# Gate and value products of a GLU layer on two fp16 parts per operand, scaled by powers of two found on the chip, in place of two rounded fp32 parts

## The chip, the cores and the metric

The kernel runs on one core of a Trainium2 chip. The metric is the device time of one execution in microseconds (us). A core has a matrix engine (PE, whose weight loads are listed apart as PEld), two engines for elementwise work (DVE and ACT), a slower one (POOL), and queues that issue transfers (here nearly all from SP). Each engine works through its own instructions in the order in which they were written; an instruction that waits holds back all those behind it on its engine.

## The reference, cut to what matters

```python
def _attn_ref(q, k, v, proj):                 # 2 batches, 8 heads, 768 rows, 64 wide
    q_bucket, k_bucket = ...                  # 6 sign bits of q @ proj and of k @ proj
    scores = np.where(q_bucket == k_bucket, scale * q @ k.T, -1e9)
    attn = softmax(scores)                    # sum(attn) + 1e-9 under the division
    return attn @ v

x = attn_out as [1536, 512]
gate = 1.0 / (1.0 + np.exp(-(x @ w_gate)))    # w_gate, w_val: 512 x 1536
val = x @ w_val
y = gate * val @ w_out                        # 1536 x 512
h = y @ w_in                                  # 512 x 2048, piecewise square, then @ w_out2
```

`w_gate` comes 188.5 times larger than `w_val` and the others, so its values need a scale before they fit an fp16 number.

## The kernel before, in words

**Attention** (0 to about 245 us) runs over 8 pairs of heads, four of batch 0 and then four of batch 1. A pair is one *unit* of some 28 us. In it PE makes the scores (`sc`), DVE takes row maxima (L473), ACT the exponentials (`P`, L477, with a read of the accumulator behind each), PE transposes (`pt`, L502), ACT makes the upper fp16 part (`PT`, L511) and DVE the lower (L514), and PE multiplies with the values (`O`, L560). The order of all engines comes from tables (`AT`, and `AM` for the last unit): `at(t, ...)` puts a step at tick t of its unit, and everything is recorded in order of ticks. Meanwhile the next pair's `q` and `k` are prepared by DMA copies on the chip (`H<-U`, `U<-W`, `W<-H`, `H<-N`, `N<-W`), which stand in SP's queue with the loads. The values of a pair, `vr`, are loaded, their absolute maximum is taken (DVE, L523, into `vm`), sent as a row to one partition (`vrow<-vm`, DMA), reduced there and turned into a power of two (DVE, L534 to L536), and sent back to all partitions (`vm<-vrow`, DMA). For the first pair PE carries the maxima there and back in place of the two transfers.

**The gate and value layer** (about 232 to 413 us) is made of 24 *quads*: 12 weight tiles g0, v0, g1, v1 to g5, v5, each for batch 0 and batch 1. The products of a tile are made by a scheme with 7 half-size products instead of 8 (`SEQ`: the seven write the PSUM banks qa, qe, qb, qa, qb, qc, qd). A product `P(i)` is 6 matmuls of 128x384: two halves of the depth, and for each `mm3`: upper by upper part, upper by lower, lower by upper. So a quad has 42 matmuls. Three *seeds* (`seed`, ACT, L254) copy one bank to another, on which a later product goes on adding: qb<-qa ahead of P(2), qc<-qb ahead of P(5), qd<-qb ahead of P(6). `keep5` (ACT) saves qe, `sum` (DVE) adds, `act` is the tanh of gate tiles (ACT, L257).

A weight tile is made ready while earlier quads run: `a_load` (1 MB of 64-bit words in three DMAs, `wr`), `a_abs` (ACT, 2), `a_conv` (5 to 6 DVE steps that build the fp32 numbers `wt`), `a_sum` (DVE, 4 steps, `ws`), `a_hi` (ACT: the rounded upper part, 128x768 and twice 128x512) and `a_lo` (DVE: the rest). Of g0, most steps are done by POOL during attention (the generator `fw`). `on(t, ...)` puts these steps at ticks t, where one tick is one product. The upper and lower parts of the layer's input are `hB`, `lB`, `hT`, `lT`.

**Afterwards** (413 to 777 us) come the `w_out` product (`o`, `y`) and the second MLP (`p`, `z`), whose PE work the change doesn't touch; the 24 splits of `h` into two parts (`on_h`) feed the first of them.

Of the kernel before, what the change touches and what calls it, by code (L numbers as in the profile page):

```python
# [22 lines left out]
VMIN = 2.0 ** -60  # L23
# [6 lines left out]
def lsh_attention_glu_act(ctx, tc, qt, kt, v, proj, w_gate, w_val, w_out1, w_in2, w_out2, ident_d, code_d, out):  # L30
# [28 lines left out]
    cst = const.tile([128, 5], F32, name="cst")  # L59

# [18 lines left out]
    def qtile(name, dt=F32R, q2=False):  # L79
        if q2:  # L80
            return Q2[0].tile([128, S], dt, tag="q2", bufs=10, name=name)
        return keep.tile([128, S], dt, tag="qk", bufs=26, name=name)
# [6 lines left out]
    def raw4(name):  # L89
        return keep.tile([128, 512], I64, tag="wr", bufs=2, name=name)  # L90
# [7 lines left out]
    XX, BO, WO, YF = {}, {}, {}, {}  # L98

# [77 lines left out]

    def a_load(t):

        raw = WO.setdefault(t, {})["raw"] = [raw4(f"wr{h}_{t}") for h in range(2)]  # L180
# [43 lines left out]
    class Quad:  # L224
# [31 lines left out]
        def tanh(self, out, x):  # L256
            nc.scalar.activation(out=out, in_=x, func=AF.Tanh, scale=0.5)  # L257
# [83 lines left out]
    with ExitStack() as actx:  # L341
# [11 lines left out]
        def load_v(b, p, eng=nc.sync):  # L353
            vr = ap.tile([128, 2, NI * D], F32, tag="vr", name=f"vr_{b}_{p}")
# [95 lines left out]
        class Unit:  # L450
# [28 lines left out]
            def ST(self):  # L479
                vm = VM[self.b, self.p]  # L480
                if self.i // GI == 0:
                    nc.gpsimd.tensor_scalar(out=vm[:, 2:3], in0=vm[:, 1:2], scalar1=1e-9, scalar2=1.0, op0=ALU.mult, op1=ALU.mult)
                nc.gpsimd.tensor_scalar(out=self.st[:, 2], in0=self.st[:, 1], scalar1=vm[:, 1:2], scalar2=vm[:, 2:3], op0=ALU.mult, op1=ALU.add)
# [32 lines left out]

        def split_v(b, p, h):
            vr = VR[b, p]
            if h == 0:
                vm = VM[b, p] = ap.tile([128, 3], F32, tag="vm", name=f"vm_{b}_{p}")  # L520
                row = ROW[p % 2]
                VS[b, p] = [row, vm]
                nc.vector.tensor_reduce(out=vm[:, 0:1], in_=vr, op=ALU.max, axis=AX.XY, apply_absolute_value=True)  # L523
                if (b, p) != seq[0]:
                    nc.sync.dma_start(row[:, 0:128], vm[:, 0:1])
            elif h == 1:
                row, vm = VS[b, p]
                u = row.bitcast(U32)
                first = (b, p) == seq[0]
                if first:  # L530
                    nc.vector.tensor_reduce(out=row[:, 130:131], in_=idle[0:1, 3, :], op=ALU.max, axis=AX.X)
                    nc.vector.tensor_scalar(out=row[:, 129:130], in0=row[:, 130:131], scalar1=VMIN, scalar2=None, op0=ALU.max)
                else:
                    nc.vector.tensor_reduce(out=row[:, 129:130], in_=row[:, 0:129], op=ALU.max, axis=AX.X)  # L534
# [863 lines left out]
```

## Time and profile before

| | |
|---|---|
| time, median of 3 runs | 778.2 us (775.28 to 778.82) |
| the profiled execution's own time | 779.02 us |
| its span on the core | 777.2 us (1.82 us lie outside it) |
| busy, share of the span: PE, DVE, ACT, POOL | 98%, 80%, 67%, 19% |
| matmuls | 4880 |

A busy share says how much of the span an engine had an instruction under way. Matmuls overlap, so PE counts as busy also where it is filled unevenly: what a matmul costs is read from the distance between the starts of two.

### The profile page before, as it was taken

The page shows a single profiled execution, that of the slowest core. Times are in us where ns is not written, and L with a number is a line of the kernel's source. Part 1 is how long each engine was busy: PE and PEld are TensorE (multiplying, and loading weights), DVE is VectorE, ACT ScalarE, POOL GpSimd, SP SyncE. Part 2 cuts the span into 40 slices and gives each one's busy share as a digit, 9 for nine tenths or more (in the row PEclk, how much of TensorE's full clock was granted, in tenths as well). Part 3 has the DMA queues.
Part 4 walks back from the last instruction along what each step waited for, and adds up shares of the span by engine and source line. Part 5 has one row for each costly group of instructions (what it writes and reads, how often), then busy time and mean ns, then how long its engine had stood idle before and what let it go on. Part 6 is the DMA issues. An engine that isn't in the chain of part 4 may idle for free.

```text
span 777.2 us, 12993 instructions
## 1 busy us (share of the span) xinstructions
PE 757.8 (98%) x4880; PEld 690.1 (89%) x4880; DVE 621.3 (80%) x1091; ACT 520.8 (67%) x1012; POOL 145.6 (19%) x168
## 2 busy tenths in 40 slices
PE   7899998999999999999999999999999999999997
PEld 4778886888878999999999999999999998888986
DVE  5889997999977977877869958888989867666643
ACT  5899897989875566566555543556666667676753
POOL 5345476664684000000000000000000000000000
PEclk9999999999999999999999999999999999999999
DMA  8645456454101131131122412433332201000002
GB/s 231 174 125 151 102 157 175 93 153 112 33 1 55 55 110 55 55 109 55 55 82 87 146 66 82 136 109 109 108 105 86 82 0 75 8 1 0 1 1 81
DMA packets 41390, 66.48 MB, mean 86 GB/s; under 512 B 5744, under 2 KB 28656, under 8 KB 41328
## 3 DMA queue, kind: packets, MB, share of 16 engines
q1 hardware_dynamic: 40592, 64.97, 28.4%
q8 instruction: 38, 0.62, 0.3%
q10 hardware_dynamic: 736, 0.69, 0.3%
q14 instruction: 24, 0.20, 0.1%
HBM read 45.58 MB, written 3.15 MB: 63 GB/s over the span
## 4 chain that ended last, share of the span: by engine, by line
PE 67%; DVE 1%; POOL 0%; ACT 0%; issue 0%; POOLq 0%
PE qa L290 3%; PE qa L289 3%; PE qa L291 3%; PE p L291 3%; PE p L289 3%; PE p L290 3%; PE qb L289 2%; PE y L289 2%; PE y L290 2%; PE y L291 2%; PE qe L289 2%; PE qe L290 2%; PE qe L291 2%; PE qb L290 2%; PE qb L291 2%; PE qa L1157 2%
## 5 line engine op out<-in xcount | busy, mean ns | idle before, releaser
L514 DVE SCALAR_TENSOR_TENSOR PT<-pt,PT 128x512 f16<-128x512 f32 x144 | 95.1, 680 | 9.1 <-ACT PT L511 8.3
L473 DVE TENSOR_REDUCE st<-sc 128x1 f32<-128x768 f32 x96 | 90.9, 947 | 8.2 <-PE sc L465 7.2
L511 ACT ACTIVATE PT<-pt 128x512 f16<-128x512 f32 x144 | 82.5, 599 | 14.5 <-PE pt L502 13.3
L477 ACT ACTIVATE P<-sc,st 128x768 f32<-128x768 f32 x96 | 87.0, 907 | 6.6 <-DVE st L473 5.9
L502 PE MATMUL pt<-ident,P 128*128 128x128 f32 x576 | 78.9, 278 | 0.8 <-DVE PT L514 0.8
L502 PEld LDWEIGHTS pt<-ident,P 128*128 128x128 f32 x576 | 65.9, 142 | 9.4 <-issue 4.7
L560 PE MATMUL O<-PT,vh 128*64 128x256 f16 x576 | 53.9, 277 | 0.0
L291 PE MATMUL p<-yh,whl_i 128*128 128x384 f32 x128 | 43.0, 336 | 0.0
L289 PE MATMUL p<-yh,whl_i 128*128 128x384 f32 x128 | 42.9, 335 | 0.0
L290 PE MATMUL p<-yl,whl_i 128*128 128x384 f32 x128 | 42.9, 335 | 0.0
L560 PEld LDWEIGHTS <-vh 128*64 128x64 f16 x576 | 31.3, 109 | 11.6 <-issue 10.3
L1134 ACT ACTIVATE t<-p,cst 128x384 f32<-128x384 f32 x32 | 18.3, 573 | 27.0 <-PE p L291 27.0
L560 PE MATMUL O<-PT,vl 128*64 128x256 f16 x288 | 33.8, 273 | 0.0
L465 PE MATMUL sc<-H,H 128*128 128x384 f32 x96 | 29.2, 385 | 3.6 <-DMA H<-N 3.3
L465 PE MATMUL sc<-N,N 128*128 128x384 f32 x96 | 29.4, 387 | 2.0 <-ACT N L403 1.0
L1139 DVE SCALAR_TENSOR_TENSOR gg<-p,t 128x384 f32<-128x384 f32 x32 | 17.7, 553 | 13.4 <-ACT t L1136 13.3
L254 ACT ACTIVATE qb<-qa 128x384 f32<-128x384 f32 x24 | 11.4, 475 | 24.1 <-PE qa L291 13.5
L254 ACT ACTIVATE qd<-qb 128x384 f32<-128x384 f32 x24 | 11.4, 475 | 23.8 <-PE qb L291 20.4
L374 POOL TENSOR_TENSOR W<-n,U 128x768 fp32r<-128x768 f32 x14 | 26.6, 1897 | 0.4
L135 ACT ACTIVATE w<-wr_i 128x512 f32<-128x512 f32 x16 | 10.7, 668 | 22.7 <-DMA wr_i<-in_moe_w_in_dram 22.6
L465 PE MATMUL sc<-U,U 128*128 128x384 f32 x96 | 25.0, 342 | 0.0
L289 PEld LDWEIGHTS p<-yh,whl_i 128*128 128x128 f32 x128 | 24.0, 188 | 0.5
(1219 smaller groups left out, 2486.6 us busy)
## 6 DMA issues: line engine op xcount, KB each, us to landing
wr_o<-in_moe_w_out_dram SPq DMA_DIRECT2D x28, 512.0 KB, 3.3
H<-U SPq DMA_DIRECT2D x28, 192.0 KB, 3.7
wr_i<-in_moe_w_in_dram SPq DMA_DIRECT2D x8, 512.0 KB, 3.9
wr_i<-in_moe_w_in_dram SPq DMA_DIRECT2D x16, 256.0 KB, 3.0
n<-in_qt_dram SPq DMA_DIRECT2D x8, 384.0 KB, 4.2
n<-in_kt_dram SPq DMA_DIRECT2D x8, 384.0 KB, 6.0
vr<-in_v_dram SPq DMA_DIRECT2D x8, 384.0 KB, 3.6
wr_g<-in_moe_w_gate_dram SPq DMA_DIRECT2D x6, 512.0 KB, 3.7
```

What stands on the lines that cost most here:

```text
L254: nc.scalar.activation(out=self.new("bcd"[m]), in_=src, func=AF.Copy)
L289: nc.tensor.matmul(ps, lhsT=wh, rhs=rh, start=first, stop=False, **kw)
L290: nc.tensor.matmul(ps, lhsT=wh, rhs=rl, start=False, stop=False, **kw)
L291: nc.tensor.matmul(ps, lhsT=wl, rhs=rh, start=False, stop=last, **kw)
L374: nc.gpsimd.tensor_tensor(out=self.t4[j][1], in0=self.nat[j], in1=f(self.t4[j][0]), op=ALU.subtract)
L465: nc.tensor.matmul(self.sc[:, n, 0:HN], lhsT=M[:, ts], rhs=K[:, n * HN:(n + 1) * HN], start=s0, stop=not s0)
L473: nc.vector.tensor_reduce(out=self.st[:, 0, self.c:self.c + 1], in_=self.sc[:, :, 0:HN], op=ALU.max, axis=AX.XY, negate=True)
L477: nc.scalar.activation(out=self.P, in_=self.sc[:, :, 0:HN], func=AF.Exp, bias=self.st[:, 0, self.c:self.c + 1], scale=1.0, accum_out=self. ...
L502: nc.tensor.transpose(self.ps[m][:, j, :], un[2 * self.n + e].P[:, a, c:c + 128], ident)
L511: nc.scalar.activation(out=self.part(0, m), in_=self.ps[m], func=AF.Copy, scale=PSCALE)
L514: nc.vector.scalar_tensor_tensor(out=self.part(1, m), in0=self.ps[m], scalar=PSCALE, in1=self.part(0, m), op0=ALU.mult, op1=ALU.subtract)
L560: nc.tensor.matmul(O_ps[r, 0:GN], lhsT=vv[m][:, e, i * D:(i + 1) * D], rhs=PT[:, l, e * NI + i, :], start=(s == 0), stop=(s == len(steps) ...
```

## The change

Both operands of the gate and value products become pairs of fp16 numbers (`qpair`, `w4pair`: upper and lower part in one tile, which takes the bytes that one fp32 part took). Therefore every weight tile gets a power of two of its own. `a_norm` (ACT, 128x1024) takes the absolute values of `wt` and adds them up per partition, `row_out` sends the 128 sums to one partition, `a_row` takes their maximum and its exponent (DVE, two instructions), makes the scale and its inverse (POOL, two) and sends both to all partitions, `a_hi` and `a_lo` multiply by the scale as they split, and `a_scale` (POOL) prepares the factor by which tanh and the splits of `h` take it out again. For g0, POOL multiplies `wt` once instead.

The values get one scale per batch. Batch 0's four loads stand at the start, ahead of g0's load, and their four maxima (`v_max`) are taken in unit 0; batch 1's loads and maxima are spread over units 0 to 3, and one row is sent there and back. The reductions and the two transfers of each later pair are gone, and units 4 to 6 have no `v_max`. The tables `QP` and `WP` set the ticks of a quad's and of a tile's steps; `QP` holds what stood there before.

```diff
@@ new functions
+    def exponents(row, mx, lead):
+        u = row.bitcast(U32)
+        m, e, inv, sc = (u[:, i:i + 1] for i in (128, 129, 130, 131))
+        nc.vector.tensor_reduce(out=row[:, 128:129], in_=mx, op=ALU.max, axis=AX.X)
+        nc.vector.tensor_scalar(out=e, in0=m, scalar1=EXP, scalar2=None, op0=ALU.bitwise_and)
+        nc.gpsimd.tensor_scalar(out=inv, in0=e, scalar1=EMIN, scalar2=(lead - 14.0) * 2.0 ** 23, op0=ALU.max, op1=ALU.add)
+        nc.gpsimd.tensor_scalar(out=sc, in0=inv, scalar1=-1.0, scalar2=254.0 * 2.0 ** 23, op0=ALU.mult, op1=ALU.add)
+    def row_out(key, x):
+        RW[key] = next(nrow)
+        nc.sync.dma_start(RW[key][:, 0:128], x)
+    def row_in(key, x, lead):
+        row = RW.pop(key)
+        exponents(row, row[:, 0:128], lead)
+        nc.sync.dma_start(x, row[:, 130:132].unsqueeze(1).broadcast_to([1, 128, 2]))
+    def a_norm(t):
+        x, raw = wsc[:, a_num(t)], WO[t]["raw"][0]
+        nc.scalar.activation(out=raw.bitcast(F32), in_=WO[t]["wt"], func=AF.Abs, accum_out=x[:, 0:1])
+        row_out(t, x[:, 0:1])
+    def a_row(t):
+        row_in(t, wsc[:, a_num(t), 2:4], 0.0)
@@ a_hi, a_lo, tanh
-        nc.scalar.activation(out=a_tile(t, "h" + g, q2)[:, cs], in_=WO[t][src][:, cs], func=AF.Copy)
+        nc.scalar.activation(out=a_tile(t, "h" + g, q2)[:, cs], in_=WO[t][src][:, cs], func=AF.Copy, scale=scale)
-        xsub(eng, a_tile(t, "l" + g, q2)[:, cs], WO[t][src][:, cs], f(WO[t]["h" + g][:, cs]))
+            nc.vector.scalar_tensor_tensor(out=lo, in0=x, scalar=a_sc(t), in1=hi, op0=ALU.mult, op1=ALU.subtract)
-            nc.scalar.activation(out=out, in_=x, func=AF.Tanh, scale=0.5)
+            nc.scalar.activation(out=out, in_=x, func=AF.Tanh, scale=a_out(self.t, self.b))
@@ attention: values
+        def v_max(b, p):
+            nc.vector.tensor_reduce(out=vmx[b][:, p:p + 1], in_=VR[b, p], op=ALU.max, axis=AX.XY, apply_absolute_value=True)
+        def v_all(b):
+            x = vmx[b]
+            nc.vector.tensor_reduce(out=x[:, NP:NP + 1], in_=x[:, 0:NP], op=ALU.max, axis=AX.X)
...
-            load_v(*seq[0], nc.sync)
+            for p in range(NP):
+                load_v(0, p, nc.sync)
             a_load("g0")
...
+                    t0 = AT["MAX"][2]
+                    for i in range(NP):
+                        at(t0 + 0.001 + 0.3 * i, 0, q, v_max, 0, i)
+                    at(t0 + 1.0, 0, q, v_all, 0)
...
+            at(14.05, 0, last, a_norm, "v0")
             at(14.1, 0, last, a_load, "g1")
@@ ticks of a tile's steps
-        on(base - (1.9 if t == 2 else 3.4), a_abs, n, 0, True)
...
+        on(base + T["norm"], a_norm, n)
+        on(base + T["row"], a_row, n)
+        on(base + T["scale"], a_scale, n)
...
-    on_split(t, 1.0, ("h", b, ORD[s]), lambda: HR[b, ORD[s]], lambda: hg(f"h{b}_{ORD[s]}"))
+    on_split(t, 1.0, ("h", b, ORD[s]), lambda: HR[b, ORD[s]], lambda: hg(f"h{b}_{ORD[s]}"), a_out(f"v{ORD[s] % F1H}", b))
```

**DVE in unit 0.** Before, behind the third score maximum of the first pair (`st<-sc`) there is one maximum of values (`vm<-vr`), and the fourth score maximum comes next:

```order
L473 TENSOR_REDUCE st_0_1_0_191<-sc_0_0_0_206 128x1
L523 TENSOR_REDUCE vm_0_216<-vr_0_175 128x1
L473 TENSOR_REDUCE st_0_1_0_191<-sc_0_0_1_227 128x1
L531 TENSOR_REDUCE vrow_93<-idle 1x1
L532 TENSOR_SCALAR vrow_93<-vrow_93 1x1
L535 TENSOR_SCALAR vrow_93<-vrow_93 1x1
L536 TENSOR_SCALAR vrow_93<-vrow_93 1x1
```

In the changed kernel the same place holds four maxima of values and one over the four:

```order
L549 TENSOR_REDUCE st_0_1_0_200<-sc_0_0_0_215 128x1
L591 TENSOR_REDUCE vmx_67<-vr_0_178 128x1
L591 TENSOR_REDUCE vmx_67<-vr_1_180 128x1
L591 TENSOR_REDUCE vmx_67<-vr_2_182 128x1
L591 TENSOR_REDUCE vmx_67<-vr_3_184 128x1
L595 TENSOR_REDUCE vmx_67<-vmx_67 128x1
L549 TENSOR_REDUCE st_0_1_0_200<-sc_0_0_1_235 128x1
L587 SCALAR_TENSOR_TENSOR PT_0_0_244<-pt_2_230,PT_0_0_244 128x4x128
L194 TENSOR_REDUCE row_71<-idle 1x1
L195 TENSOR_SCALAR row_71<-row_71 1x1
```

Three 128x768 reductions and one short one now stand between the third and the fourth score maximum.

**SP at the start.** Before, one load of values stands ahead of g0's three weight loads (`wr_g`) and the two copies `H<-U` for pair 1:

```order
L355 DMA vr_0_175<-in_v_dram 128x2x384
L183 DMA wr_g_177<-in_moe_w_gate_dram 128x4x128
L185 DMA wr_g_178<-in_moe_w_gate_dram 128x2x128
L186 DMA wr_g_178<-in_moe_w_gate_dram 128x2x128
L443 DMA H_0_1_148<-U_0_1_146 64x768
```

In the changed kernel there are four:

```order
L431 DMA vr_0_178<-in_v_dram 128x2x384
L431 DMA vr_1_180<-in_v_dram 128x2x384
L431 DMA vr_2_182<-in_v_dram 128x2x384
L431 DMA vr_3_184<-in_v_dram 128x2x384
L252 DMA wr_g_186<-in_moe_w_gate_dram 128x4x128
L254 DMA wr_g_187<-in_moe_w_gate_dram 128x2x128
L255 DMA wr_g_187<-in_moe_w_gate_dram 128x2x128
L519 DMA H_0_1_151<-U_0_1_149 64x768
```

Three loads of 384 KB moved ahead of the weights and of pair 1's copies.

**ACT in a gate tile's two quads** (g1 for batch 0, then the head of batch 1). Before, the second seed (`qc<-qb`) is followed by the first tanh (`h<-qa`) and the third seed (`qd<-qb`); the value tile's upper parts (`ha_v`, `hs_v`) stand between later steps:

```order
L254 ACTIVATE qc_3992<-qb_3974 128x384
L257 ACTIVATE h_1_3965<-qa 128x384
L254 ACTIVATE qd_4011<-qb_3974 128x384
L257 ACTIVATE h_1_3965<-h_1_3965 128x384
L214 ACTIVATE ha_v_4027<-wt_v_3934 128x768
```

In the changed kernel, batch 0's quad has the value tile's norm (128x1024) between the second seed and the tanh:

```order
L330 ACTIVATE qc_3968<-qb_3944 128x384
L213 ACTIVATE wr_v_3790,wsc<-wt_v_3845 128x1024
L333 ACTIVATE h_1_3935<-qa,wsc 128x384
L330 ACTIVATE qd_3988<-qb_3944 128x384
```

And batch 1's quad has two upper parts there:

```order
L330 ACTIVATE qc_4044<-qb_4024 128x384
L284 ACTIVATE a_v_4052<-wt_v_3845,wsc 128x768
L284 ACTIVATE s_v_4054<-ws_v_3966,wsc 128x512
L333 ACTIVATE h_1_4015<-qa,wsc 128x384
L330 ACTIVATE qd_4065<-qb_4024 128x384
```

So what ACT does between the second and the third seed grew by one long instruction in one quad and by two in the other.

## Rows read from the trace of the kernel before

**Rows 1.** Page, part 1: busy time of each engine.

```profile
PE 757.8 (98%) x4880; PEld 690.1 (89%) x4880; DVE 621.3 (80%) x1091; ACT 520.8 (67%) x1012; POOL 145.6 (19%) x168
```

**Rows 2.** Window of four quads: length, busy time (instructions), clock, DMA share, GB/s.

```profile
280.00:309.10 29.10, 29.10 (x170) 29.10 (x169) 23.20 (x42) 17.12 (x34) 0.00 (x0) 1.00 0.23 73
```

**Rows 3.** Timeline of PE and PEld in a quad: start, length, instruction.

```profile
284.42 0.33 PE L289 MATMUL qb<-hT,hs_v 128*128 128x384 f32 x1
...
285.46 0.33 PE L289 MATMUL qa<-hB,ha_v 128*128 128x384 f32 x1
...
284.59 0.19 PEld L291 LDWEIGHTS qb<-hT,ls_v 128*128 128x128 f32 x1
```

**Rows 4.** Warming matmuls of bf16: timeline, durations by source line, and their window.

```profile
4.47 1.30 PE L615 MATMUL idle<-bt 128*128 128x384 bf16 x7
...
L615 PEld LDWEIGHTS <-bt x25: 96/147/151, 1.1 to 14.1; 128*128 128x128 bf16 x25
L615 PE MATMUL idle<-bt x25: 326/497/543, 1.1 to 14.4; 128*128 128x384 bf16 x25
...
4.40:5.00 0.60, 0.60 (x6) 0.34 (x5) 0.04 (x1) 0.53 (x1) 0.00 (x0) 1.00 1.10 279
```

**Rows 5.** Timeline of PE: fp16 matmuls of the values, two side by side.

```profile
102.85 0.28 PE L560 MATMUL O<-PT,vl 128*64 128x256 f16 x2
...
103.40 0.28 PE L560 MATMUL O<-PT,vh 128*64 128x256 f16 x2
```

**Rows 6.** Windows of one unit each in attention, columns as in rows 2.

```profile
57.80:86.00 28.20, 27.85 (x266) 23.21 (x266) 27.92 (x48) 24.99 (x52) 13.42 (x17) 1.00 0.53 135
114.00:142.00 28.00, 24.72 (x222) 21.01 (x220) 21.45 (x35) 22.22 (x47) 15.18 (x18) 0.94 0.65 171
```

**Rows 7.** Tiles of the values: count, ns min/median/max, first and last start.

```profile
L523 DVE TENSOR_REDUCE vm<-vr x8: 939/942/944, 16.9 to 192.5; 128x1 f32<-128x768 f32 x8
...
L535 DVE TENSOR_SCALAR vrow<-vrow x8: 141/142/142, 19.1 to 200.6; 1x1 uint32<-1x1 uint32 x8
...
DMA to landing us min/median/max: 1.9/2.4/5.1
```

**Rows 8.** Timeline of DVE in unit 0, with the idle time ahead.

```profile
16.94 0.94 DVE L523 TENSOR_REDUCE vm<-vr 128x1 f32<-128x768 f32 x1
17.80 0.95 DVE L473 TENSOR_REDUCE st<-sc 128x1 f32<-128x768 f32 x1
...
26.02 0.69 DVE L514 SCALAR_TENSOR_TENSOR PT<-pt,PT 128x512 f16<-128x512 f32 x1 [1.21 <-ACT PT L511]
```

**Rows 9.** Window of the start, columns as in rows 2.

```profile
12.00:16.00 4.00, 3.73 (x16) 2.52 (x15) 2.75 (x3) 2.48 (x5) 3.83 (x4) 0.68 0.98 322
```

**Rows 10.** Timeline of PE and DVE where unit 4 begins.

```profile
120.32 0.94 PE L465 MATMUL sc<-H,H 128*128 128x384 f32 x2 [3.28 <-DMA H<-N]
...
119.78 0.28 DVE L534 TENSOR_REDUCE vrow<-vrow 1x1 f32<-1x129 f32 x1 [2.62 <-DMA vrow<-vm]
```

**Rows 11.** ACT in the quads: timeline.

```profile
285.65 0.47 ACT L254 ACTIVATE qc<-qb 128x384 f32<-128x384 f32 x1 [0.55 <-PE qb L291]
287.73 0.47 ACT L254 ACTIVATE qd<-qb 128x384 f32<-128x384 f32 x1 [1.60 <-PE qb L291]
288.12 0.84 ACT L214 ACTIVATE ha_g<-wt_g 128x768 fp32r<-128x768 f32 x1
```

**Rows 12.** ACT by source line: count, ns min/median/max, first and last start.

```profile
L214 ACT ACTIVATE hs_v<-ws_v x12: 626/626/635, 249.3 to 394.2; 128x512 fp32r<-128x512 f32 x12
...
L477 ACT ACTIVATION_READ_ACCUMULATOR P<-sc,st x96: 189/202/272, 14.7 to 228.6; 128x1 f32 x96
...
L1134 ACT ACTIVATE t<-p,cst x32: 561/568/586, 516.5 to 639.1; 128x384 f32<-128x384 f32 x32
```

**Rows 13.** Timeline of ACT at the end of attention.

```profile
237.39 0.49 ACT L257 ACTIVATE h<-qa 128x384 f32<-128x384 f32 x1 [0.58 <-PE qa L291]
...
248.53 0.84 ACT L214 ACTIVATE ha_v<-wt_v 128x768 fp32r<-128x768 f32 x1
```

More of the change, by code (lines that the diff above doesn't have):

```diff
@@ L22 @@
 PSCALE = 2.0 ** 12
-VMIN = 2.0 ** -60
+EMIN = 67.0 * 2.0 ** 23
+EXP = 0x7F800000
 TINY = 1.2e-38
@@ L59, in lsh_attention_glu_act @@
     cst = const.tile([128, 5], F32, name="cst")
+    vmx = [const.tile([128, 8], F32, name=f"vmx{b}") for b in range(B)]
+    xinv = const.tile([128, B], F32, name="xinv")
+    wsc = const.tile([128, 2 * (F1 // 2), 8], F32, name="wsc")
+    rows = [const.tile([1, 136], F32, name=f"row{i}") for i in range(3)]
     def constants():
@@ L515, in LO, with v_row, v_scale @@
                 free.append(self.bt[m])
+        def v_max(b, p):
[3 more added lines that the diff above has]
+            nc.vector.tensor_reduce(out=x[:, NP:NP + 1], in_=x[:, 0:NP], op=ALU.max, axis=AX.X)
+            if b == 0:
+                nc.tensor.transpose(idle[0:1, 3, :], x[:, NP:NP + 1], ident)
+            else:
+                row_out("x", x[:, NP:NP + 1])
+        def v_row(b):
+            if b == 0:
+                exponents(rows[0], idle[0:1, 3, :], 2.0)
+                nc.tensor.matmul(idle[:, 2, 0:2], lhsT=ones, rhs=rows[0][:, 130:132], start=True, stop=True)
+            else:
+                row_in("x", vmx[b][:, NP + 2:NP + 4], 2.0)
+        def v_scale(b):
+            if b == 0:
+                nc.scalar.copy(out=vmx[b][:, NP + 2:NP + 4], in_=idle[:, 2, 0:2])
+            nc.gpsimd.tensor_copy(out=xinv[:, b:b + 1], in_=vmx[b][:, NP + 2:NP + 3])
         def split_v(b, p, h):
@@ L519, in split_v @@
             if h == 0:
[L520 to L525, printed above, removed]
-            elif h == 1:
[L527 to L534, printed above, removed]
-                nc.vector.tensor_scalar(out=u[:, 130:131], in0=u[:, 129:130], scalar1=0x7F800000, scalar2=None, op0=ALU.bitwise_and)
-                nc.vector.tensor_scalar(out=u[:, 132:133], in0=u[:, 130:131], scalar1=-1.0, scalar2=268.0 * 2.0 ** 23, op0=ALU.mult, op1=ALU.add)
-                if not first:
-                    nc.sync.dma_start(vm[:, 1:2], row[:, 132:133].broadcast_to([1, 128]))
-                    VS[b, p][1] = vm[:, 1:2]
-            elif h == 2:
-                nc.gpsimd.tensor_scalar(out=vr, in0=vr, scalar1=VS[b, p][1], scalar2=1.0, op0=ALU.mult, op1=ALU.mult)
-            elif h == 3:
@@ L588, in first_weights @@
                     yield
+                a_norm("g0")
+                yield
+                a_row("g0")
                 a_load("v0")
+                yield
+                wt = WO["g0"]["wt"]
+                nc.gpsimd.tensor_scalar(out=wt, in0=wt, scalar1=a_sc("g0"), scalar2=1.0, op0=ALU.mult, op1=ALU.mult)
                 for m in range(4):
@@ L607, in lsh_attention_glu_act @@
             constants()
-            ROW = [ap.tile([1, 134], F32, tag=f"vrow{i}", bufs=1, name=f"vrow{i}") for i in range(2)]
-            for row in ROW:
-                nc.vector.memset(row[:, 128:129], VMIN)
             idle = pA.tile([128, 4, 128], F32, tag="pv", bufs=PVB, name="idle")
@@ L615, in warm @@
                     nc.tensor.matmul(idle[:, 0:3], lhsT=bt[:, 0:128], rhs=bt, start=True, stop=True)
-            def scale_out():
-                nc.tensor.transpose(idle[0:1, 3, :], VS[seq[0]][1][:, 0:1], ident)
-            def scale_in():
-                nc.tensor.matmul(idle[:, 2, 0:1], lhsT=ones, rhs=VS[seq[0]][0][:, 132:133], start=True, stop=True)
-            def scale_keep():
-                vm = VM[seq[0]]
-                nc.scalar.copy(out=vm[:, 1:2], in_=idle[:, 2, 0:1])
-                VS[seq[0]][1] = vm[:, 1:2]
             warm(18)
@@ L1225, in lsh_attention_glu_act @@
+        for i, g in enumerate("abcd"):
+            on(s0 + T["sum"][i], q_op, k, "sum", g)
+            on(s0 + T["act"][i] + (1.0 if k == 1 and g == "a" else 0.0), q_op, k, "act", g)
     for t in range(2, NT):
         base, n = 14 * (t - 1), name(t)
+        T = WP[n if n in WP else n[0]]
         if t > 2:
-            on(base - 9.0, a_load, n)
-        on(base - (1.9 if t == 2 else 3.4), a_abs, n, 0, True)
-        on(base - 1.4, a_abs, n, 1, True)
-        for m, d in enumerate((0.1, 0.9, 1.7, 2.4, 3.0, 3.6)):
+            on(base + T["load"], a_load, n)
```

167 lines of the change are left out of this document (109 added, 58 removed).

## The prediction

> **What bounds the kernel now.** I read three views. First the busy time of each engine: PE has work under way in 98% of the span [rows 1]. That alone would mislead, since an average covers stages with different limits, so the windows of single stages come next. In the gate and value layer, four quads take 29.10 us, and in all of that time PE and PEld are busy at a granted clock of 1.00 (2.4 GHz), while DVE has 23.2 us of work and ACT 17.1 [rows 2]. Three more windows of the same length, up to 396.4 us, read alike. So this stage lasts as long as its matmuls, and a cheaper matmul shows in the time at once. A unit of attention is another matter: in 28.2 us DVE has 27.92 us of work, PE 27.85 and ACT 24.99 [rows 6]. There three engines wait for each other in turn, and work taken from one of them comes back only in part. The third view, the timeline, gives the prices below. The layers after 413 us have the same matmuls before and after.
>
> **The matmuls: −10.6 us.** In a quad, PE starts seven matmuls between 284.42 and 285.46 us: six steps, 173.3 ns each [rows 3]. What an fp16 matmul of the same shape (128x384) takes is not shown, but two rows come near. The warming matmuls are 128x384 in bf16, a format as wide as fp16, each with a weight load: seven from 4.47 us take 1.30 us, the last of them 326 ns, so the starts lie (1.30 − 0.326) / 6 = 162.3 ns apart, at a clock of 1.00, and a load takes 96 ns where the fp32 one takes 190 [rows 3, 4]. The fp16 matmuls of the values do 256 columns in 110 ns ((103.40 − 102.85) / 5) [rows 5]; 384 columns at that rate are 165 ns. I take the first, being of the same shape: 11.0 ns × 42 matmuls = 0.46 us a quad. 23 of the 24 quads lie in the stage that PE bounds (the first lies in attention's tail), so 23 × 0.46 = 10.6 us. The bounds: 8.0 us at 165 ns, and nothing if the format makes no difference.
>
> The Trainium skill ("TensorE: Matmul & The Clock Gate", section "Back-to-back issue gap") gives for an isolated warm stream N/2.4 + 2.5 ns whatever the format, which for 384 columns is 162.5. The bf16 rows agree with it; the fp32 rows, at 173.3, do not. By that rule alone the matmuls would cost the same before and after and the sum below would end near 781 in place of 770.5.
>
> **Seeds in the quads: +1.3 us (0 to 3).** The first thing that can take the gain back is ACT, which works in order. A tick becomes 6 × 0.162 = 0.97 us. I count from the start of P(2) (284.42). The second seed starts 0.19 us after P(2) ends, as it does now (285.65 against 284.42 + 1.04) [rows 3, 11]: 1.16, and ends at 1.63. In batch 1's quad of a gate tile there then come the value tile's parts, 0.84 and 0.63 us [rows 11, 12], and the tanh, 0.49 [rows 13], each with a scale that is now read from memory. Such an operand has its nearest row in the rectifier with a bias from memory: 0.568 us for 128x384, against 0.47 for a plain copy [rows 11, 12], so 0.09 each. That makes 1.63 + 0.93 + 0.72 + 0.58 + 0.47 = 4.33 for the third seed's end, and P(6) wants it at 4 × 0.974 = 3.90. Neighbours on ACT overlap (288.12 is 0.08 before 287.73 + 0.47 [rows 11]), so some 0.33 of the lateness goes away: PE waits 0.1 to 0.43 us, once for each of v1 to v5. Middle 0.26 × 5 = 1.3 us. In batch 0's quad the norm stands there: 128x1024 with an accumulator. It is not shown; below it lies the 128x768 part (0.84) with the read of an accumulator (0.2), above it two 128x512 parts (1.26) with that read [rows 11, 12], so 1.04 to 1.46. With 1.25 the third seed ends at 1.63 + 1.25 + 0.58 + 0.47 = 3.93 less overlaps, just in time, so nothing; with both ends and the chain's other steps I keep 0 to 3 us for the stage.
>
> Hidden by the rest of this stage: DVE gains per four quads two row reductions and two 1x1 steps, 2 × (0.28 + 0.14) = 0.8 us [rows 7, 10], and ACT two norms and the scales, some 3.5; DVE has 5.9 us free and ACT 12.0 [rows 2]. The lower parts become one instruction of the same length class (0.69 for 128x512 [rows 8]). POOL does nothing there [rows 2], so the short scales are free. Without that cover the DVE steps would cost 0.8 × 5 = 4 us. The splits of h with a scale add 24 × 0.09 = 2.2 us to an ACT that has a third of the span free [rows 1].
>
> **Start of attention: +2.7 us (1.4 to 3.7).** Between the third and the fourth score maximum DVE has one maximum of values now; the next instruction follows 0.86 us after its start (17.80 − 16.94) [rows 8]. Three more cost 2.6 us and the short one over four columns about 0.1. Behind them wait the fourth score maximum, then ACT's exponential, then PE's transposes. DVE is idle later for 1.21 us, waiting for ACT [rows 8]; ACT would be just as late, so I don't subtract it, but 2.6 − 1.2 = 1.4 is the lower bound. At the same time three loads of 384 KB move ahead of g0's weights and of pair 1's copies. The transfers are full there (0.98 of their time, 322 GB/s [rows 9]), so each takes 1.2 us: 3.7 us for the copies that the next pair's first scores need. The two delays run side by side and aren't added.
>
> **Units 1 to 6: −2.1 us.** Units 1 and 2 lose the row's three DVE steps, 0.28 + 2 × 0.14 = 0.56 each [rows 7, 10], with the two transfers: 1.1 us, of which I count half, as PE has 27.85 of 28.2 us [rows 6]: −0.6. Units 4 to 6 lose the value maximum as well: 3 × (0.86 + 0.56) = 4.3 us of DVE [rows 7, 8]; half again, −2.3 with the transfers gone from SP's queue (0 to −4.3). Unit 3 keeps everything, and gets g0's norm on ACT and its row. Where unit 4 begins, PE waits 3.28 us for a copy `H<-N` and DVE 2.62 us for the row, both landing behind 1 MB of v0's weights [rows 10]; that window has 24.72 us of PE work in 28 [rows 6]. That load still stands there, three queue places from those copies, so I let the wait stay, and add +0.8 (0 to 1.5) for a norm of 1.25 us on an ACT that is nearly as full as the others.
>
> **End of attention: +1.0 us (0.3 to 2.5).** v0's norm comes behind the first tanh (237.39) [rows 13], and then its row goes out, is reduced, and comes back, each transfer 2.4 us, or 5.1 behind a large load [rows 7]; here g1's 1 MB stands between them. 237.9 + 1.25 + 2.4 + about 1 + 5.1 = 247.7 at least, and DVE's reduction stands ahead of attention's last steps. v0's upper parts start at 248.53 now [rows 13]; I count on 0.5 to 1.5 us later.
>
> **The sum.** −10.6 + 1.3 + 2.7 − 0.6 − 2.3 + 0.8 + 1.0 = −7.7 us. The profiled execution takes 779.02 us (span 777.2 and 1.82 outside it), so 771.3; the median shown is 0.8 lower, so **770.5 us**.
>
> **The rivals.** *The format makes no difference* (0.08). For it speaks that the row of another format is only seven matmuls long; against it, that the fp16 rows give 165 too. Then the 10.6 is gone: 781, no change.
> *The new steps on ACT and the rows take most of the gain back* (0.16). ACT's order leaves the third seed at 3.9 to 4.3 ticks' worth of time where 3.90 is wanted, and a wait of 0.4 us in each of 23 quads, say because another seed falls behind a norm or a tanh too, costs 8 us beyond the 1.3: 775 to 779, within 0.5%.
> *Attention gives back all that DVE loses* (0.16). DVE is the fullest engine of a unit [rows 6]. Then units 4 to 6 bring 4.3 and the wait of rows 10, with the row's small transfers no longer among the copies, shrinks by 1 to 2: 770.5 − 2.0 − 2 = 766.5, with a shorter start 764.
> *Slower* (0.10). Every `a_row` stands on DVE in order and waits for its row. If a row lands after 5.1 us, as the slowest one did, in place of 2.4 (the median) [rows 7], DVE stands still for 2.7 us, and behind it wait the sums that free PE's banks. DVE's spare time is (5.9 − 0.8) / 2 = 2.5 us a tile, but not where the wait is; if PE loses 1.5 us a tile, 11 tiles cost 16.5: 787. It ends above the time before from 0.7 us a tile on (7.7 / 11), and above 0.5% slower from 1.05.
>
> **How the numbers follow.** The forecast has the rest, 0.50, and its own range is 767 to 774 (±3.5 from the start, the end and the seeds). A measurement of this kernel can tell about 0.5%, 3.9 us, from no change: below 774.3 is faster, above 782.1 slower. Faster: 0.50 + 0.16, and 0.02 of the second rival's near end: 0.68. Same: 0.08 + 0.14 = 0.22. Slower: 0.10. From 764 to 780 all of the forecast and of the third rival, the second, and a part of the first lie inside; what is left out is the last one and the rest of the first.
>
> **What would show it.** In the changed kernel's timeline of PE: starts of fp16 matmuls 162 to 165 ns apart, and windows of four quads of 27.3 us plus 0.1 to 0.4 us of PE waiting for ACT's qd. At the start: the fourth score maximum (now at 17.80) near 20.5. In units 4 to 6: DVE's work 1.4 us less each, the unit 0.7 shorter. At v0: its upper parts at 249 to 250. I would be wrong above all if the starts lay 173 ns apart, if PE waited in every quad, or if the chain of maxima at the start moved the rest by less than 1 or more than 4 us.

## The result and the profile after

The changed kernel takes 782.33 us (median of 6 runs, 780.99 to 784.06), the kernel before 776.74 in the 6 runs now at hand: a ratio of 1.0069, with a 95% interval from 1.0048 to 1.0090. It is slower by 0.7%, where 7.7 us less (770.5) was forecast and the range ended at 780. The profiled execution took 782.72 us with a span of 780.9; that of before, 779.02.

First the step on which the forecast rested. The page's busy times, which answer to [rows 1]:

```profile
PE 752.0 (96%) x4880; PEld 614.8 (79%) x4880; DVE 626.2 (80%) x1094; ACT 539.6 (69%) x1036; POOL 155.5 (20%) x203
```

And the timeline of PE in a quad, to set beside [rows 3]:

```profile
293.00 0.33 PE L367 MATMUL qc<-pB,s_v 128*128 128x384 f16 x1
293.17 0.33 PE L365 MATMUL qd<-pT,a_v 128*128 128x384 f16 x1
293.33 0.33 PE L366 MATMUL qd<-pT,a_v 128*128 128x384 f16 x1
293.49 0.33 PE L367 MATMUL qd<-pT,a_v 128*128 128x384 f16 x1
```

Three steps in 0.49 us: an fp16 matmul starts every 163 ns, where the fp32 one took 173. The cheaper matmul is there. It isn't in the time. The windows of [rows 2], and one with more in it, show why:

```profile
280.00:309.10 29.10, 28.13 (x172) 16.63 (x171) 24.40 (x47) 20.21 (x40) 2.69 (x8) 1.00 0.23 73
...
338.20:367.30 29.10, 26.90 (x165) 15.87 (x163) 23.63 (x46) 19.00 (x37) 1.85 (x5) 1.00 0.24 73
```

PE was busy in all of these 29.10 us before. Now it stands still for 1 to 2.2 us of each window. The waits of PE from the end of attention to the end of the quads (225 to 420 us), each with what it waited for, the sum, the number and the longest:

```profile
PE qb L365 <- ACT qb L330: 6.0, 9, 1.5
PE qd L365 <- ACT qd L330: 1.4, 2, 1.3
PE qa L365 <- ACT a_g L284: 1.2, 1, 1.2
PE qb L365 <- ACT qc L330: 0.8, 2, 0.5
PE pt L575 <- DVE PT L587: 0.8, 2, 0.5
PE qa L367 <- DVE a_g L294: 0.7, 1, 0.7
```

Apart from `pt`, which stood there before, these are waits for seeds and for a gate tile's parts: 10.1 us, where the same list of before has 1.3 (0.95 for ACT's qb and 0.3 for POOL's hT). The list is short of the loss: it counts a wait only from the end of the matmul drawn ahead of it, and that end lies 0.17 us behind the place where the next could have started (0.33 us long, 163 ns apart). The starts give all of it. Here is the first matmul of a quad's second product (`qe`), in the second quad and in the last, before and then after:

```profile
245.02 0.47 PE L289 MATMUL qe<-hT,hs_g 128*128 128x384 f32 x1
407.13 0.33 PE L289 MATMUL qe<-hT,hs_v 128*128 128x384 f32 x1
...
246.74 0.33 PE L365 MATMUL qe<-pT,s_g 128*128 128x384 f16 x1
410.73 0.33 PE L365 MATMUL qe<-pT,s_v 128*128 128x384 f16 x1
```

These 22 quads take 162.11 us before and 163.99 after. A quad in which PE never waits takes 7.28 us before and 6.825 after (42 matmuls, 173.3 and 162.5 ns apart), so 22 × 0.455 = 10.0 us are saved. The rest is lost: 1.9 us before and 13.8 after, 11.9 more. Of the 13.8, 7.4 us fall in the 18 quads from the sixth on, where nothing was lost before, and 6.4 in the four ahead of them, where 1.9 were.

What goes wrong in a steady quad is in ACT's timeline (start, length, instruction):

```profile
286.74 1.04 ACT L213 ACTIVATE wr_g<-wt_g 128x1024 f32<-128x1024 f32 x1
287.68 0.19 ACT L213 ACTIVATION_READ_ACCUMULATOR wr_g<-wt_g 128x1 f32 x1
287.78 0.60 ACT L333 ACTIVATE h<-h,wsc 128x384 f32<-128x384 f32 x1
288.28 0.56 ACT L333 ACTIVATE h<-qd,wsc 128x384 f32<-128x384 f32 x1
288.75 0.47 ACT L330 ACTIVATE qb<-qa 128x384 f32<-128x384 f32 x1
```

The *next gate* tile's norm stands among the tanh steps that end a gate tile's second quad, and the first seed of the next quad comes behind all of them. The matmul behind it waited, 0.54 us by the list and 0.70 by the distance of its start from the one before:

```profile
289.27 0.32 PE L365 MATMUL qb<-pT,s_v 128*128 128x384 f16 x1 [0.54 <-ACT qb L330]
```

I had put the value tile's norm and parts into the sum, and not this one.

The start lost more than forecast. DVE, then ACT, to set beside [rows 8], and PE's first scores of pair 1 (at 37.51 before):

```profile
16.50 3.52 DVE L591 TENSOR_REDUCE vmx<-vr 128x1 f32<-128x768 f32 x4
20.06 0.16 DVE L595 TENSOR_REDUCE vmx<-vmx 128x1 f32<-128x4 f32 x1
...
21.11 0.90 ACT L553 ACTIVATE P<-sc,st 128x768 f32<-128x768 f32 x1 [3.01 <-DVE st L549]
...
20.27 0.27 PE L597 MATMUL idle<-ident,vmx 128*1 128x128 f32 x1 [1.12 <-DVE vmx L595]
22.65 0.58 PE L604 MATMUL idle<-row,ones 1*128 1x2 f32 x2 [1.68 <-POOL row L197]
...
43.01 0.42 PE L541 MATMUL sc<-H,H 128*128 128x384 f32 x1
...
24.00:26.00 2.00, 2.00 (x11) 0.56 (x10) 0.69 (x1) 1.61 (x4) 0.87 (x2) 0.50 1.07 389
```

The fourth score maximum, behind the four, came at 20.13 in place of 17.80, as worked out (2.3 us). But pair 1 began 5.5 us late. The last row, a window, shows what else there is: PE runs at a granted clock of 0.50 (1.2 GHz) from 15.4 to 18.8 us and again, behind the two waits, from 22.2 to 29.1. The first of these stretches begins ahead of the waits, and the three other profiled kernels with this start (experiments 2 to 4) have a clock of 1.00 there; it falls once in each, from 20 to 22 us on, and they begin pair 1 at 41.96 to 42.51, so 4.5 to 5.0 us late. And one part went better: PE waits 1.51 us for `H<-N` at unit 4 in place of 3.28 [rows 10].

### The profile page after: what moved, and what is told of

The parts are those of the page before. It is cut to its first block, busy times and chain, and to the rows that moved or that the text cites. A ratio compares the mean times of both kernels' runs of the same rounds, so it can differ in the third digit from the quotient of the medians.

```text
span 780.9 us, 13074 instructions
## 1 busy us (share of the span) xinstructions
PE 752.0 (96%) x4880; PEld 614.8 (79%) x4880; DVE 626.2 (80%) x1094; ACT 539.6 (69%) x1036; POOL 155.5 (20%) x203
## 3 DMA queue, kind: packets, MB, share of 16 engines
q1 hardware_dynamic: 42320, 64.98, 28.2%
## 4 chain that ended last, share of the span: by engine, by line
PE 56%; ACT 6%; DVE 2%; DMA 1%; issue 1%; POOL 0%; ACTq 0%; DVEq 0%
PE p L367 3%; PE p L365 3%; PE p L366 3%; PE y L365 2%; PE y L366 2%; PE y L367 2%; PE qa L367 2%; PE qa L366 2%; PE qa L365 2%; PE qa L1233 2%; PE qa L1232 2%; PE qe L1232 2%; PE qe L1233 2%; PE qa L1231 2%; PE qe L1231 2%; PE o L1232 2%
## 5 line engine op out<-in xcount | busy, mean ns | idle before, releaser
L635 PEld LDWEIGHTS <-vh 128*64 128x64 f16 x576 | 31.3, 109 | 11.8 <-issue 10.3
L196 POOL TENSOR_SCALAR row<-row 1x1 uint32<-1x1 uint32 x14 | 3.7, 264 | 119.3 <-DVE row L195 119.3
L365 PEld LDWEIGHTS p<-yh,whl_i 128*128 128x128 f32 x128 | 24.0, 188 | 0.5
L366 PEld LDWEIGHTS p<-yl,whl_i 128*128 128x128 f32 x128 | 24.0, 188 | 0.5
L367 PEld LDWEIGHTS p<-yh,whl_i 128*128 128x128 f32 x128 | 24.0, 188 | 0.0
```

Of the source, the lines that this page charges most:

```text
L365: nc.tensor.matmul(ps, lhsT=wh, rhs=rh, start=first, stop=False, **kw)
L366: nc.tensor.matmul(ps, lhsT=wh, rhs=rl, start=False, stop=False, **kw)
L367: nc.tensor.matmul(ps, lhsT=wl, rhs=rh, start=False, stop=last, **kw)
L635: nc.tensor.matmul(O_ps[r, 0:GN], lhsT=vv[m][:, e, i * D:(i + 1) * D], rhs=PT[:, l, e * NI + i, :], start=(s == 0), stop=(s == len(steps) ...
```

## The experiments

**1. The values as before.** The attention part of the change undone (`load_v`, `split_v` with its own row for each pair, PE's row for the first pair); `xinv` is 1.

```diff
-            for p in range(NP):
-                load_v(0, p, nc.sync)
+            load_v(*seq[0], nc.sync)
...
-                        at(t0 + 0.001 + 0.3 * i, 0, q, v_max, 0, i)
...
+                    vs[:2] = AT["MAX"][2] + 0.001, AT["MAX"][3] + 0.001
```

> The fp16 products and the tables of the change, but the values scaled per pair of heads as before (the factor per batch that tanh takes out is then a constant 1). Theory 'start': the four maxima and the row at the start cost the 5.5 us by which pair 1's first scores came later, and 2.3 us of that came back where units 4 and 5 begin; so undoing this part brings about 3 us: 779. Pair 1's scores begin near 37.5 us again, and PE waits 3 us for H<-N at unit 4 again. Rival 'the quads alone': the start's delay is absorbed by attention's end, so nothing changes by more than 1 us: 782.

775.93 us (10 runs), 0.9989 of the time before [0.9976, 1.0002], so 6.4 us below the changed kernel. Pair 1's scores begin here:

```profile
37.07 0.42 PE L543 MATMUL sc<-H,H 128*128 128x384 f32 x1
```

The lead over the changed kernel is 5.94 us there, the same when unit 3 begins (96.24 against 90.30), and 6.2 us when the quads do. So the start's loss is never given back, and units 4 to 6, which lost 4.3 us of DVE work, gained nothing by it: from unit 4's first scores to unit 7's it is 78.89 us in the changed kernel and 78.83 here. The shorter wait at unit 4 is there as well (1.3 us): it isn't the values that shortened it. By SP's order it is v0's load, which now stands behind g0's row and so behind one of the two copies; no run moved that load alone. Both my expectation (3 us) and its rival (none) were too small.

**2 and 3. The quads without the search, and with the norm alone.** In the second the norm stays, and the row and its two transfers are left out as well as the DVE and POOL steps.

```diff
     def constants():
+        nc.gpsimd.memset(wsc[:, :, 2:4], 1.0)
...
     def a_norm(t):
-        x, raw = wsc[:, a_num(t)], WO[t]["raw"][0]
-        nc.scalar.activation(out=raw.bitcast(F32), in_=WO[t]["wt"], func=AF.Abs, accum_out=x[:, 0:1])
-        row_out(t, x[:, 0:1])
+        pass
     def a_row(t):
-        row_in(t, wsc[:, a_num(t), 2:4], 0.0)
+        pass
```

```diff
     def constants():
+        nc.gpsimd.memset(wsc[:, :, 2:4], 1.0)
...
-        row_out(t, x[:, 0:1])
     def a_row(t):
-        row_in(t, wsc[:, a_num(t), 2:4], 0.0)
+        pass
```

> The changed kernel without the search for the weights' powers of two: no norm, no row, no transfers, a constant scale of 1 read from the same memory operands. Theory 'chain': the norm on ACT and the wait for the row stand ahead of seeds and cost most of the 8.7 us that PE lost in the quads; without them the stretch from the second quad to the end of the quads shrinks from 171.3 to about 164 us and the time falls by 6 to 8: 775. Rival 'operands': the scale operands and the places of the upper parts in ACT's order are to blame; then at most 2 us come back: 780 to 782.

> The changed kernel with the norm on ACT but without the row (no transfers, no DVE and POOL steps; constant scale). Within the theory 'chain' it tells the norm from the row. If the norm's place on ACT is the price, PE still waits 0.54 us for the first seed behind it in each of five quads, and the gain over the changed kernel is 3 to 4 us (779); if the wait for the row is the price, nearly all of what the kernel without the search gains is here too (within 1 us of it).

Without the search: 775.84 us, 0.9979 [0.9966, 0.9992]; with the norm alone 779.12, 1.0020 [1.0003, 1.0037]. The 22 quads take 158.73 and 162.33 us (163.99 in the changed kernel). In both runs PE's granted clock is 0.50 for 3.4 us in the first quads (271.0 to 274.4 and 272.8 to 276.2), behind waits much like those of the changed kernel, where the clock stayed at 1.00; so the 18 quads from the sixth on compare better. They take 123.57 us without the search, 127.02 with the norm alone and 130.24 in the changed kernel: the norms cost 3.45 us and the rows 3.2, and the medians of the times agree (3.3 and 3.2). (The expectation's stretch reaches to the first matmul of the `w_out` product; it is 171.3 us in the changed kernel, 166.1 and 169.7 here.) The kernel without the search has this window of four quads, with PE busy throughout and 180 matmuls in it where 170 stood:

```profile
280.00:309.10 29.10, 29.10 (x180) 17.49 (x179) 24.84 (x46) 19.31 (x38) 0.00 (x0) 1.00 0.23 73
```

With the norm alone, PE's waits between 276 and 408 us are four for the first seed:

```profile
PE qb L365 <- ACT qb L330: 2.3, 4, 0.6
```

The rival that blamed the scale operands falls: both kernels still read them, and without the search hardly a wait is left in the steady quads (0.3 us by the list).

**4. The same work, re-timed.** Nothing is taken out; six entries in two rows of the table of ticks move.

```diff
-        "g": {... "norm": -1.456, "row": 1.893, "scale": 7.914, ... "hi": (6.968, 7.625, 8.56), "lo": (7.021, 8.161, 9.79)},
+        "g": {... "norm": 1.0, "row": 4.5, "scale": 9.0, ... "hi": (8.05, 9.0, 10.05), "lo": (8.9, 10.1, 11.0)},
-        "v": {... "hi": (10.245, 10.388, 12.351), ...},
+        "v": {... "hi": (10.245, 12.0, 12.9), ...},
```

> The changed kernel, complete, with three rows of the table of ticks altered: the norm of a gate tile after the first seed of the next quad in place of ahead of it, its row and upper parts 1 to 2.5 ticks later, and the value tile's half-size upper parts behind the third seed. Theory 'order': what PE loses are places in ACT's order, not ACT's work, so PE's waits in the steady quads (0.12 + 0.54 + 0.3 to 1.5 us in four quads) go and the time falls by 4 to 5: 778. Rival 'work': ACT and the rows are simply too long; the waits turn up behind other instructions and the time stays within 1 us of 782.

776.78 us, 1.0002 [0.9987, 1.0016]: 5.6 us less than the changed kernel, a little more than expected. PE's waits between 276 and 408 us:

```profile
PE qb L365 <- ACT qb L330: 0.4, 1, 0.4
PE qb L365 <- ACT qc L330: 0.3, 1, 0.3
```

The 18 quads from the sixth on take 124.66 us, 5.6 less than in the changed kernel with all its work, and 1.1 more than without the search. So it is order and not work. It isn't ACT's order alone, though: with the gate tile's row later, the value tile's 1 MB load stands ahead of the outgoing row, no longer between it and the scale that comes back, and the ten scales of these quads land after 2.32 to 2.44 us, where in the changed kernel those of g2 to g5 took 2.8 to 4.1. Experiments 3 and 9 hold the two shares apart.

**5 and 6. The clock at the start, and the row's steps on DVE.** One execution each.

```diff
+                    at(t0 + 0.999, 0, q, warm, 4)
                     at(t0 + 1.0, 0, q, v_all, 0)
+                    at(AT["T"][1] + 0.0005, 0, q, warm, 6)
```

```diff
-    def exponents(row, mx, lead):
+    def exponents(row, mx, lead, eng=nc.gpsimd):
...
-                exponents(rows[0], idle[0:1, 3, :], 2.0)
+                exponents(rows[0], idle[0:1, 3, :], 2.0, nc.vector)
```

> The changed kernel with ten more warming matmuls, four and six of them, where PE waits at the start for the maxima and for the row. They do no work that is used. Theory 'clock': the start lost 5.5 us and not 2.7 because PE, left idle by the maxima, fell to 1.2 GHz (granted clock 0.50 from 16 to 18 and from 24 to 28 us); if PE is kept busy the clock stays up and pair 1's first scores come 2 us earlier, near 41. Rival 'row': the loss lies in the waits of the chain itself; the clock rises but pair 1's scores stay at 42.5 to 43.5.

> The changed kernel, but the first row's two steps on POOL are done by DVE, as they were before the change. Theory 'row': PE waits 1.68 us for POOL there; on DVE the two steps take 0.3 us in place of 0.7, and pair 1's first scores come 0.5 to 1 us earlier: 42.2. Rival 'maxima alone': ACT's exponential, 3 us late behind the four maxima, sets the pace, and nothing moves: 43.0.

With the warming matmuls the run took 778.25 us, and pair 1 began at 40.22, 2.8 us earlier than in the changed kernel and 1.7 to 2.3 earlier than in the three others with its start (41.96 to 42.51), whose clock fell only once. Profiles with one start and one clock differ by up to 1.3 us at pair 1 (36.10 to 37.41 in the three with the values as before), so the size is rough. And not all of the 4.1 us below the median is the start's: the 22 quads, which these matmuls don't touch, took 162.7 us here in place of 164.0. The windows from 14 to 38 us of the changed kernel and of this one:

```profile
14.00:38.00 24.00, 18.95 (x94) 14.56 (x94) 16.86 (x27) 15.43 (x33) 9.42 (x15) 0.79 0.76 215
```

```profile
14.00:38.00 24.00, 18.84 (x127) 14.18 (x127) 19.39 (x30) 16.42 (x34) 9.44 (x15) 1.00 0.79 210
```

The busy time of PE is equal, the matmuls are 94 and 127, ten of them the added ones: the clock is 0.79 in one and 1.00 in the other. In the three others with this start it is 0.86. The waits of the chain stay (0.96 and 1.11 us). With the row on DVE the run took 781.68 us and pair 1 began at 41.96, as in experiment 4 where POOL does the steps: it says nothing either way.

**7. The maxima spread.** One value maximum behind each of four steps, the row later and on DVE.

```diff
-                        at(t0 + 0.001 + 0.3 * i, 0, q, v_max, 0, i)
-                    at(t0 + 1.0, 0, q, v_all, 0)
+                        at((t0 + 0.001, 1.92, 2.72, 3.40)[i], 0, q, v_max, 0, i)
+                    at(3.42, 0, q, v_all, 0)
...
+                    at(4.27, 0, q, v_row, 0)
```

> The changed kernel with the first batch's four maxima spread: one behind each of the score maxima and lower parts that follow, the row later and on DVE, so that no score maximum waits for more than one of them. The loads stand as in the change. Theory 'maxima in front of a score maximum': pair 1's first scores come at 39.5 to 40.5, 2.5 to 3.5 us earlier than in the changed kernel, and the time falls as much: 779. Rival 'loads': the three loads ahead of pair 1's copies set the start; then it stays near 43.

Pair 1 began at 39.95, 3.1 us earlier (in three more kernels with this start at 40.78 to 42.19), and yet the time is 782.16, 1.0071 [1.0056, 1.0086]. Part of the 3.1 is the clock, which was at 0.50 for 3.4 us here and for 10.3 in the changed kernel. The other three have it there for 6.8 us, as have the three others with the start of the change (41.96 to 42.51), so the spread itself brought some 1 us, no more than such profiles scatter. The gain was lost again at 350 us, where ACT, then PE, wait; the two issues on SP that matter stand first:

```profile
343.58 0.46 SPq L255 DMA_DIRECT2D wr_v<-in_moe_w_val_dram  x1
...
345.06 0.51 SPq L209 DMA_DIRECT2D wsc<-row  x1
...
350.22 0.93 ACT L284 ACTIVATE a_g<-wt_g,wsc 128x768 f16<-128x768 f32 x1 [2.67 <-DMA wsc<-row]
...
352.74 0.32 PE L365 MATMUL qb<-pT,s_v 128*128 128x384 f16 x1 [2.53 <-ACT qb L330]
...
353.40:356.80 3.40, 3.40 (x12) 1.65 (x11) 2.58 (x5) 0.78 (x2) 0.00 (x0) 0.50 0.00 0
```

The last row is a window: behind this wait PE's granted clock is 0.50 for 3.4 us, in which matmuls start 320 ns apart. That costs 1.7 us more, beside 2.7 for the wait itself (the changed kernel lost 1.7 and no clock in the same place). A gate tile's scale comes back behind the next value tile's 1 MB. Issued at 345.06, it landed 5.1 us later; in the changed kernel the slowest took 4.1. Two runs put this to the test.

**8 and 9. The load behind the scale, and well ahead of it.**

```diff
-        "v": {"load": -13.148, "abs": (-8.736, -6.094), ...
+        "v": {"load": -12.09, "abs": (-7.8, -6.094), ...      # the first
+        "v": {"load": -18.5, "abs": (-8.736, -6.094), ...     # the second
```

> The kernel with the spread start, in which the value tile's 1 MB load is issued one tick later, behind the transfer that brings a gate tile's scale back, and not ahead of it (its first absolute values 0.9 tick later). Theory 'queue': the 3 us that the spread start won were lost again in the quads because the scale's few bytes landed behind 1 MB (5.1 us after their issue in place of 2.3 to 2.9), ACT waited for them with a gate tile's upper part, and the next seed stood behind it; with the scale ahead of the load PE's waits for the first seed fall by 3 to 4 us in all: 778.5. Rival 'ACT's own work': the wait moves to another instruction and the time stays at 782.

> The kernel with the spread start, with the value tile's 1 MB load 5.4 ticks earlier and nothing else moved: it then stands ahead of the gate tile's outgoing row, which leaves the queue empty when the scale comes back, and it can't be late for its absolute values. In the run that had the scale ahead of the load, the scale landed 2.33 us after its issue each time, but ACT then waited 2.3 to 2.9 us for the load, which stood later. Theory 'queue': the scale lands in 2.33 us again, ACT waits under 1 us for it, PE's waits for the first seed behind it fall from up to 2.5 us to 0.2 to 0.3 each, and the time is 778 to 779. Rival 'no queue': the time stays at 782.

The first took 792.65 us, 1.0202 [1.0182, 1.0222], the slowest of all. The scales of the steady quads did land 2.3 us after their issue, but ACT waited for something new between 276 and 408 us, and PE behind it:

```profile
ACT wt_v L156 <- DMA wr_v<-in_moe_w_val_dram: 11.2, 5, 2.9
```

```profile
PE qb L365 <- ACT qb L330: 12.2, 8, 2.8
```

Behind two of these waits the clock fell as well (0.50 from 297.8 to 301.2 and from 393.4 to 396.8). The expectation missed this: one tick later, the load was late for its absolute values, which stand on ACT ahead of a seed too. The second, which avoids that, took 777.61 us, 1.0009 [0.9997, 1.0021], 4.6 us less than the kernel that it is made from, though its start happened to be 2.2 us later in the profile; the 18 quads from the sixth on take 127.82 us, 4.9 less. The ten scales of the quads landed after 2.32 to 2.44 us, and of PE's waits those behind the norm are left:

```profile
PE qb L365 <- ACT qb L330: 2.2, 4, 0.5
PE qd L365 <- ACT qd L330: 0.2, 1, 0.2
```

**10 to 12. The repairs put together.** Experiments 1 and 4 in one; the same with the first quads re-timed (v0's half-size parts and g1's absolute values behind the third seed, g1's row earlier); and the change with values per batch, spread start and all re-timing.

```diff
-        on(10.057 + 2.0 * m, a_hi, "v0", "s", m, True)
+        on(12.0 + 0.9 * m, a_hi, "v0", "s", m, True)
...
-        "g1": {"abs": (-1.624, -2.928), "conv": (-1.428, -0.628, 0.127, ...), "row": 7.227, "hi": (12.461, 12.377, 14.087) ...
+        "g1": {"abs": (-1.9, -1.3), "conv": (-0.7, -0.5, 0.127, ...), "row": 6.4, "hi": (11.99, 12.377, 14.087) ...
```

> The values as before and the re-timed quads together, the fp16 products complete with their search. If the two losses are independent, the gains add: 775.93 less the 5.55 that re-timing brought is 770.4, which is 0.991 of the time before. If they are not, because attention's end hides one of them, it stays above 773.

> The values as before, re-timed quads, and the steps of v0 and g1 in the first quads re-timed too: v0's half-size upper parts and g1's absolute values behind the third seed, g1's row 0.8 tick earlier and its full-size upper part ahead of the half-size one. PE loses 5 us there (1.26 + 1.36 for seeds, 1.17 + 0.73 for g1's parts, 0.5 for a copy). If order is the cause there as well, 2 to 4 us come back: 767 to 769. If the transfers set it, it stays at 770 to 771.

> The change complete, values per batch included, with all repairs: maxima spread at the start, quads and first quads re-timed. By the sums of what each repair brought (3.1 at the start, 5.5 in the quads, 2 to 4 in the first quads) it lands at 770 to 772, some 2 to 3 us behind the same kernel with values per pair, because three maxima more and a row still stand at the start. If units 4 to 6 do gain from the absent maxima, it is level with it: 768.

The first took 770.78 us, 0.9915 [0.9898, 0.9933]: the gains add, and this version beats both kernels. Re-timing the first quads brought nothing (771.43, 0.9928 [0.9913, 0.9943]); the waits there went to other places:

```profile
PE qb L367 <- ACT qb L332: 2.1, 2, 1.7
PE qe L369 <- DVE s_g L296: 1.8, 1, 1.8
```

With values per batch and every repair it is 776.74 us, 0.9992 [0.9978, 1.0006], 5.3 us behind the same kernel with values per pair, more than the 2 to 3 expected: pair 1 begins at 40.78 against 37.41, and its clock is at 0.50 from 24.3 to 31.1 us, where the other's stays at 1.00.

## Why the prediction was wrong, point by point

**The matmuls** were right: 163 ns between starts, and windows of 180 matmuls once nothing stands in the way.

**Seeds in the quads, "+1.3 us (0 to 3)"**, is the step that failed: by the starts, PE loses 11.9 us more than before. The mechanism, ACT's order ahead of a seed, was the right one, and the place that I costed came out as worked out: P(6) is 0.27 to 0.33 us late in four quads and 0.1 in a fifth, 1.3 us together. But I followed one seed in two quads, and not every new instruction to the next seed behind it. What I left out: the next gate tile's norm ahead of the first seed of the following quad (0.70 us in four quads and 0.24 in a fifth, 3.1 in all; experiments 3 and 4), the wait for a scale that comes back behind 1 MB, with a seed behind that wait (0.36 to 1.7 us in four quads, 3.1 in all; experiments 7 to 9), and 4.5 us in the first quads. Of these last it is known what PE waits for (seeds, g1's parts), not why it is late: neither taking the search out nor re-timing those steps brought them back. "DVE has 5.9 us free and ACT 12.0" was true and beside the point: experiment 4 removes nearly all the waits of the steady quads with the same work. The second rival (0.16, 775 to 779) had this mechanism at 8 us beyond the 1.3, where 10.6 were measured. The last one (0.10) had a late transfer in it, but the row, with DVE behind it; the rows of the quads landed after 1.9 us each, and it was the scale, with ACT behind it.

**"Start of attention: +2.7 us (1.4 to 3.7)"** was mis-sized: 5.5 in the profiled execution, 4.5 to 5.0 in three others. The delay on DVE came out as worked out, 2.3 us at the fourth score maximum. What was missing is PE's clock: left idle by the chain, it fell to 1.2 GHz, and the one run that kept it up began pair 1 1.7 to 2.3 us earlier than those with this fall alone. The other fall in the changed kernel's profile, at 15.4 us, came ahead of the chain, and no run shows it to be the change's. What is left of the loss in the run that kept the clock up, 40.22 − 37.07 = 3.2 us against the values as before, is near the term. [Rows 9] had shown a clock of 0.68 in the start of the kernel before, and I read past it. The share of the three loads wasn't tried by itself; the warmed run keeps them, so it can be at most a part of the 3.2.

**"Units 1 to 6: −2.1 us"** met its number, −2.2 from unit 1's first scores to unit 7's, by luck: its parts were wrong. Units 1 and 2 took 0.1 us more, not 0.6 less. By experiment 1, units 4 to 6 gained nothing from the absent maxima; from unit 5's first scores to unit 7's it is 52.09 us before (147.96 to 200.05) and 52.21 after. In [rows 6] I took DVE's 27.92 of 28.2 us, in an earlier unit, for the bound. A later window, most of it unit 6, before and in the changed kernel:

```profile
170.00:198.00 28.00, 28.00 (x272) 23.66 (x271) 26.28 (x43) 25.43 (x52) 12.34 (x17) 1.00 0.43 107
...
170.00:198.00 28.00, 28.00 (x275) 23.43 (x273) 25.02 (x39) 25.12 (x52) 13.65 (x17) 1.00 0.39 93
```

PE is busy for all of it, as it was before; DVE's share of it could fall without moving the end. Unit 3, on the other hand, didn't lose 0.8: units 3 and 4 together gained 2.4 us, with the load that made PE wait pushed back in SP's order. Behind the longer wait of before, PE's clock was 0.50 from 120.4 to 123.8 us; after, it stays at 1.00 there.

**"End of attention: +1.0 us"** had the wrong sign: unit 7 begins 3.3 us late and the second quad 1.7, so attention's end gained 1.6 us, and no run looked into why. The quads behind it then fell back by 2.7 (the sixth begins 4.4 late). The sum of both is near the term by luck, the places aren't.

**The sum** in the prediction's terms, by the times at which each stretch begins in the two profiles: matmuls −10.0, waits in the quads +11.9, start +5.5, units 1 to 6 −2.2, end of attention −1.6, together +3.6 of the 3.7 us between the two profiled executions. The median of before lies 2.3 us below its profiled execution, that of the changed kernel 0.4 below its own, which makes the 5.6. Against the −7.7 of the prediction, the quads' waits account for 10.6 us and the start for 2.8; the end of attention went the other way by 2.6.

## What to carry to other kernels

Where one engine bounds a stage and another hands it something in fixed order, spare time on that other engine is no cover: follow each added instruction to the next hand-over behind it, in every period of the pattern, and count a wait on a transfer there as if it stood on the bound engine itself. Put such work right behind a hand-over, not ahead of one, and a small transfer that such work waits for not right behind a large load; here the two together turned 782 into 777 us with the same instructions. And a gain that a profile promises for a filled engine holds only in the units where no other engine is just as full.

## What was not expected of the hardware

Part of what the start lost is PE's clock, and it can be had back by work that nobody needs: with ten idle matmuls the mean granted clock between 14 and 38 us is 1.00, where it is 0.79 in the changed kernel and 0.86 in three others with its start, and pair 1 begins 1.7 to 2.3 us earlier than in those three (one run). The transfer that brings a scale back took 2.3 to 2.4 us in the quads where no load stood just ahead of it in SP's queue, 2.7 to 3.0 behind a 1 MB load for g2, g3 and g5, and 4.1 and 5.1 for g4 (the changed kernel and experiment 7); what made that one longer is open. And a wait of PE can cost more than itself: behind the one of 2.5 us at 350 us the clock was 0.50 for 3.4 us, 1.7 us more.
